# Engine programs emitted straight into the main program instead of inside a block

## The chip, the core and the metric

The kernel runs on one core of a Trainium2 chip. The core has five engines, each with its own instruction stream: the matrix engine (PE; its weight loads are shown as PEld), the vector engine (DVE), the scalar engine (ACT), GpSimd (POOL) and the sync engine (SP), which here issues nearly all transfers. The engines run by themselves and wait for each other through semaphores. The metric is the device time of one execution of the program in microseconds, as the median of several runs; lower is better.

## The reference

Sixteen tiles of 128 tokens (2048 tokens, width 512) go through two branches whose results are mixed by a gate. Branch A is attention with 32 heads of width 16 in four segments of 512 tokens, causal inside a segment, and a linear memory carried from one segment to the next. Branch B is a gated feed-forward layer with 1792 hidden units.

```python
x = A_x
g = _sigmoid((x * gate_w).sum(-1, keepdims=True))
a = _A_ref(x, A_wq, A_wk, A_wv, A_wo, A_beta)
b = _B_ref(x, B_W_gate, B_W_up, B_W_down)
return g * a + (1 - g) * b
...
for s in range(N):
    logits = jnp.einsum('bhqd,bhkd->bhqk', qs, ks) * scale + mask
    p = _softmax(logits, axis=-1)
    a_dot = jnp.einsum('bhqk,bhkd->bhqd', p, vs)
    pq = phi(qs)
    a_mem = num / den
    o = g * a_mem + (1.0 - g) * a_dot
    M = M + jnp.einsum('bhld,bhle->bhde', pk, vs)
    z = z + jnp.einsum('bhld->bhd', pk)
...
gate = gate * (gate > 0)
h = gate * up
return jnp.einsum('bsf,fd->bsd', h, W_down)
```

## The kernel before

The kernel is made in two steps. First `program` describes the whole computation as operations with the tiles that they read and write, and a list scheduler (`Sched.run`) decides, at build time, which engine does each operation and in which order; the outcome is one list per engine, `sc.prog[e]`, of two kinds of items: a wait for a semaphore's value, and an instruction that raises a semaphore when it is done. Second, `Sched.emit` walks the five lists and writes the instructions. All weights lie in SBUF; the four segments are worked through in order, with the projections (L791, L793), the attention scores and their weighted sums (L913, L969), the feed-forward products (L1043, L1082) and the output projection (L1075) interleaved on PE.

The change touches the second step alone. Before, `build_kernel` opens a block (L576) and hands it to `emit` (L577 calls it); `emit` gets one section of the block for each engine (`block.tensor`, `block.scalar` and so on) and writes each engine's list into its section (L540). What the reader needs of the surroundings:

- Ahead of the block stands an opening that every program of this kind has. It is attributed to L1188, where the program object is made: POOL sets four constants, every engine drains and raises one semaphore, POOL collects the four of them and raises another, and the four engines then go on.
- Entering the block gives each engine a jump from the main program to its own section (L540). Leaving the block gives each engine a jump to a common end section, and in it a closing meeting of the same make as the opening one: each engine drains and raises a semaphore, POOL waits for four of these and raises a second semaphore by four, and each of the others waits for one of the four. All of this is attributed to L576.
- The last thing in SP's list, written at the end of `program` (L1166 to L1168), is a wait for each of the 16 semaphores that count landed transfers. A wait is written by L534. Two waits fit in one instruction; in the kernel before, the sixteenth, for the semaphore of the last output store, is carried by SP's jump to the end section.
- The last stores to the output are issued by SP (L1094) from the tile `osb`, which ACT (L1092) and DVE (L1091) fill from the last products of PE (L1075, L1082).

Of the kernel before, what the change touches and what calls it, by code (L numbers as in the profile page):

```python
# [128 lines left out]
class Sched:  # L129
# [395 lines left out]
            self.place(op, e, start)  # L525
            self.relax = False

    def emit(self, block):
        sec = {"pe": block.tensor, "act": block.scalar, "dve": block.vector, "pool": block.gpsimd, "sp": block.sync}
        for e in self.ENGS:  # L530
            def body(engobj, prog=self.prog[e], e=e):
                for item in prog:
                    if item[0] == "wait":
                        engobj.wait_ge(self.sem[item[1]], item[2])  # L534
                    else:
                        _, op, st, inc = item
                        res = op.fns[e](engobj)
                        for r in (res if op.nd > 1 else [res]):
                            r.then_inc(self.sem[st], inc)
            sec[e](body)  # L540


def plan(S, D, F):
    NT, KT, NF = S // 128, D // 128, F // 128
    return [
        ("xT", [128, KT, XR * 512], BF16), ("wq", [128, KT, 512], BF16), ("wk", [128, KT, 512], BF16), ("wv", [128, KT, 512], BF16),
        ("wo", [128, 4, 512], BF16), ("wg", [128, KT, F], BF16), ("wu", [128, KT, F], BF16), ("wd", [128, NF - SBX, 512], BF16),
        ("qT", [128, QTN, 512], BF16), ("kT", [128, 4, 512], BF16), ("kp", [128, 5, 8, 128], BF16),
        ("phiq", [128, 4, 512], BF16), ("ek", [128, EKN, 512], BF16), ("phik", [128, 4, 512], BF16), ("ttmp", [128, 2, 512], BF16),
        ("vaug", [128, 2, 4, 32, 17], BF16), ("vsh", [128, 4, 32, 17], BF16), ("E", [128, NBLK * 512], BF16),  # L550
        ("Tn", [128, TNN, 512], F32), ("adT", [128, 512], BF16), ("oTt", [128, 512], BF16),
        ("amem", [128, 2, 512], BF16), ("amemT", [128, 4, 512], BF16), ("oT", [128, OTN, 512], BF16),
        ("hT", [128, HTN, 512], BF16), ("rl", [128, 3, 512], BF16), ("osb", [128, 3, 512], BF16),
        ("Mc", [128, 4, 68], F32), ("Mbd16", [128, 4, 136], BF16), ("mumask", [128, 4, 136], F32),
        ("braw", [128, 32], BF16), ("eb", [128, 32], F32), ("romgh", [128, 32], F32), ("epsv", [128, 32], F32),
        ("gexp", [128, NT], F32), ("omg", [128, NT], F32), ("gexpT", [128, NT * 4], F32), ("gwb", [128, 512], BF16),  ("gl", [128, NT], F32),
        ("rden", [128, 64], F32), ("rdg", [128, 64], F32), ("rdm", [128, 128], F32), ("pm8", [128, 8], F32), ("pm", [128, 2], F32), ("ident", [128, 128], BF16),
    ]


def build_kernel(nc, A_x, A_wq, A_wk, A_wv, A_wo, A_beta, W_g, W_u, W_d, gate_w, out):
    _, S, D = A_x.shape
    F = W_g.shape[1]
    assert D == 512 and S % 512 == 0 and F % 128 == 0
    NSEG, KT, NF, NT = S // 512, D // 128, F // 128, S // 128
    EPS, SCALE = 1e-6, 16 ** -0.5
    sc = Sched(seeds=(237719, 74891, 0, 89398, 0, 53401, 416309, 0, 0, 0, 710933, 0, 718714, 120896, 538430, 820480, 585027, 870794, 793690, 0, 589972, 0, 0, 0, 454998, 16783, 0,))
    T = {}
    with contextlib.ExitStack() as stack:
        for name, shape, dt in plan(S, D, F):  # L570
            T[name] = stack.enter_context(nc.sbuf_tensor(name, shape, dt))
        PS = stack.enter_context(nc.psum_tensor("ps", [128, 8, 512], F32))
        for st in sc.streams:
            sc.sem[st] = stack.enter_context(nc.semaphore(f"s_{st}"))
        program(sc, nc, T, PS, A_x, A_wq, A_wk, A_wv, A_wo, A_beta, W_g, W_u, W_d, gate_w, out, NSEG, KT, NF, NT, EPS, SCALE)
        with nc.Block() as block:  # L576
            sc.emit(block)  # L577
    return sc


# [590 lines left out]
def bass_gated_mix__memory_aug_infini_attn__glu_gated_reglu__prompt_kernel(  # L1171
    nc, A_x, A_wq, A_wk, A_wv, A_wo, A_beta, B_x, B_W_gate, B_W_up, B_W_down, gate_w, out
):
    return build_kernel(nc, A_x, A_wq, A_wk, A_wv, A_wo, A_beta, B_W_gate, B_W_up, B_W_down, gate_w, out)
# [28 lines left out]
```

## Time and profile before

| | before |
|---|---|
| median of three runs | 264.14 us |
| lowest, highest run | 264.01, 264.25 us |
| span of the profiled execution | 262.7 us |
| instructions recorded | 6432 |
| PE busy | 255.7 us, 97% of the span |
| ACT, DVE, POOL busy | 184.5, 179.1, 131.0 us |
| granted TensorE clock over the span | 1.000 |

The span reaches from the first to the last of the program's own instructions, the opening at L1188 and the closing at L576 included. What the launch does before and after it lies outside the span and inside the metric. Instructions of an engine's queue (waits, drains, jumps, transfers issued) have a `q` behind the engine's name and do not count as busy.

### The profile page before, as it was taken

The page shows a single profiled execution, that of the slowest core. Times are in us where ns is not written, and L with a number is a line of the kernel's source. Part 1 is how long each engine was busy: PE and PEld are TensorE (multiplying, and loading weights), DVE is VectorE, ACT ScalarE, POOL GpSimd, SP SyncE. Part 2 cuts the span into 40 slices and gives each one's busy share as a digit, 9 for nine tenths or more (in the row PEclk, how much of TensorE's full clock was granted, in tenths as well). Part 3 has the DMA queues.
Part 4 walks back from the last instruction along what each step waited for, and adds up shares of the span by engine and source line. Part 5 has one row for each costly group of instructions (what it writes and reads, how often), then busy time and mean ns, then how long its engine had stood idle before and what let it go on. Part 6 is the DMA issues. An engine that isn't in the chain of part 4 may idle for free.

```text
span 262.7 us, 6432 instructions
## 1 busy us (share of the span) xinstructions
PE 255.7 (97%) x2619; PEld 114.6 (44%) x2653; DVE 179.1 (68%) x356; ACT 184.5 (70%) x160; POOL 131.0 (50%) x295
## 2 busy tenths in 40 slices
PE   8999999999999999999999999999999999999996
PEld 5444443444443544334444544443444444344444
DVE  5488878789986587778788676757667716477600
ACT  4586689999789779785768787677777665676021
POOL 3036557564646466666555457836365354545100
PEclk9999999999999999999999999999999999999999
DMA  6989646930261134213040242010131101000011
GB/s 197 286 302 281 138 66 148 274 44 22 68 155 25 24 81 117 48 22 33 10 107 13 59 91 23 4 40 2 31 76 40 22 24 34 26 2 2 0 42 40
DMA packets 34925, 19.87 MB, mean 76 GB/s; under 512 B 24016, under 2 KB 34128, under 8 KB 34896
## 3 DMA queue, kind: packets, MB, share of 16 engines
q1 hardware_dynamic: 34800, 19.46, 30.4%
q8 instruction: 21, 0.34, 0.6%
q14 instruction: 8, 0.07, 0.1%
q10 hardware_dynamic: 96, 0.00, 0.0%
HBM read 10.40 MB, written 2.11 MB: 48 GB/s over the span
## 4 chain that ended last, share of the span: by engine, by line
PE 97%; issue 1%; DVE 1%
PE ps L1043 38%; PE ps L1082 19%; PE ps L793 11%; PE ps L913 9%; PE ps L969 6%; PE ps L791 5%; PE ps L1075 5%; PE ps L856 1%; PE ps L693 1%; PE ps L707 1%; PE ps L836 0%; DVE hT L1054 0%; DVE Tn L979 0%; DVE osb L746 0%; DVE osb L1091 0%
## 5 line engine op out<-in xcount | busy, mean ns | idle before, releaser
L935 POOL TENSOR_SCALAR_AFFINE_SELECT E<-E 64x256 bf16<-64x256 bf16 (+1 forms) x256 | 111.1, 445 | 111.9 <-ACT E L929 82.7
L929 ACT ACTIVATE E<-ps 128x2048 bf16<-128x2048 f32 x72 | 135.1, 1876 | 38.7 <-PE ps L913 38.6
L1043 PE MATMUL ps<-xT,wu 128*128 128x512 bf16 x213 | 57.2, 380 | 1.4 <-issue 1.3
L1043 PE MATMUL ps<-xT,wg 128*128 128x512 bf16 x219 | 57.7, 380 | 0.6 <-issue 0.3
L1082 PE MATMUL ps<-wd,hT 128*128 128x512 bf16 (+2 forms) x229 | 52.8, 367 | 0.9 <-issue 0.6
L1054 DVE TENSOR_TENSOR hT<-ps,rl 128x512 bf16<-128x512 f32 x56 | 38.5, 687 | 16.5 <-PE ps L1043 16.4
L1082 PEld LDWEIGHTS ps<-wd,hT 128*128 128x128 bf16 x238 | 21.4, 98 | 23.8 <-issue 2.4
L1043 PEld LDWEIGHTS ps<-xT,wg 128*128 128x128 bf16 x224 | 20.6, 98 | 25.7 <-issue 2.8
L1043 PEld LDWEIGHTS ps<-xT,wu 128*128 128x128 bf16 x224 | 20.1, 98 | 25.4 <-issue 3.5
L913 PE MATMUL ps<-qT,kp 32*128 32x192 bf16 (+7 forms) x512 | 28.6, 287 | 0.0
L979 DVE STREAM_TRANSPOSE Tn<-ps 128x512 f32<-128x512 f32 x32 | 21.3, 696 | 9.1 <-PE ps L969 9.1
L1052 DVE TENSOR_SCALAR rl<-ps 128x512 bf16<-128x512 f32 x30 | 20.7, 690 | 8.2 <-PE ps L1043 7.9
L1091 DVE TENSOR_SCALAR osb<-ps,omg 128x512 bf16<-128x512 f32 (+1 forms) x8 | 5.6, 700 | 26.0 <-PE ps L1082 15.1
L1051 ACT ACTIVATE rl<-ps 128x512 bf16<-128x512 f32 x26 | 15.5, 598 | 9.9 <-PE ps L1043 9.7
L913 PEld LDWEIGHTS ps<-qT,kp 32*128 32x128 bf16 x512 | 8.2, 92 | 25.3 <-issue 13.1
L969 PE MATMUL ps<-E,vaug 64*17 64x128 bf16 (+7 forms) x512 | 18.7, 283 | 0.0
L969 PE MATMUL ps<-E,vsh 64*17 64x128 bf16 (+7 forms) x512 | 18.3, 283 | 0.0
L1092 ACT ACTIVATE osb<-ps,omg 128x512 bf16<-128x512 f32 (+1 forms) x9 | 6.1, 675 | 16.4 <-PE ps L1075 14.0
L793 PE MATMUL ps<-xT,wq 128*128 128x512 bf16 x61 | 16.1, 391 | 0.4 <-issue 0.3
L1075 PE MATMUL ps<-wo,oT 128*128 128x512 bf16 (+2 forms) x67 | 16.2, 366 | 0.2 <-issue 0.2
L793 PE MATMUL ps<-xT,wk 128*128 128x512 bf16 x60 | 15.6, 380 | 0.4 <-issue 0.3
L791 PE MATMUL ps<-wv,xT 128*128 128x512 bf16 x63 | 15.3, 380 | 0.1
(68 smaller groups left out, 229.2 us busy)
## 6 DMA issues: line engine op xcount, KB each, us to landing
vsh<-vaug SPq DMA_DIRECT2D x8, 272.0 KB, 4.3
osb<-in_A_x_dram SPq DMA_DIRECT2D x16, 128.0 KB, 2.3
out_dram<-osb SPq DMA_DIRECT2D x15, 128.0 KB, 1.7
wg<-in_B_W_gate_dram SPq DMA_DIRECT2D x8, 224.0 KB, 5.0
wu<-in_B_W_up_dram SPq DMA_DIRECT2D x8, 224.0 KB, 5.9
wd<-in_B_W_down_dram SPq DMA_DIRECT2D x1, 1792.0 KB, 10.5
hT<-in_A_x_dram SPq DMA_DIRECT2D x2, 256.0 KB, 3.0
wq<-in_A_wq_dram SPq DMA_DIRECT2D x4, 128.0 KB, 3.3
```

Of the source, the lines that this page charges most:

```text
L791: ins = e.matmul(A(ep)[:, :], lhsT=V.xT[:, kt, tok + col * 128:tok + (col + 1) * 128], rhs=w[:, kt, :], start=(kt == 0), stop=(kt == KT - 1))
L793: ins = e.matmul(A(ep)[:, :], lhsT=w[:, kt, col * 128:(col + 1) * 128], rhs=V.xT[:, kt, tok:tok + 512], start=(kt == 0), stop=(kt == KT - 1))
L913: ins = q.matmul(dst, lhsT=V.kp[r, kslot(s, G), c, :], rhs=V.qT[r, qslot(s, G), q0:q0 + w], start=True, stop=True, tile_position=(32 * jj, ...
L929: acts.append(act(lambda a: a.activation(V.E[:, base * 512:base * 512 + min(2048, 4 * W)], PF[:, 0:min(2048, 4 * W)], ACT.Exp, scale=SCALE ...
L935: pools.append(pool(lambda g, ap=ap, lim=lim, pat=pat: g.affine_select(out=ap, in_=ap, compare_op=ALU.is_ge, fill=0.0, base=lim, pattern=[ ...
L969: ins = q.matmul(A(eps[p])[32 * jj:32 * jj + 17, 64 * (c + u):64 * (c + u + n)], lhsT=v[:, 8 * G + 2 * jj + p, :], rhs=V.E[r, f:f + 64 * n ...
L979: ds.append(dve(lambda e, p=p, ep=eps[p]: e.transpose(V.Tn[:, 2 * (G % (TNN // 2)) + p, :], A(ep)[:, :]), t_dve(512), writes=[f"Tn{2 * (G ...
L1043: ins = e.matmul(A(ep)[:, :], lhsT=w[:, kt, f * 128:(f + 1) * 128], rhs=V.xT[:, kt, c % XR * 512:(c % XR + 1) * 512], start=(kt == 0), sto ...
L1052: ("dve", lambda e, ep=eg, r=r: e.tensor_scalar(V.rl[:, r, :], A(ep)[:, :], 0.0, None, ALU.max), t_dve(512))],
L1054: evs.append(dve(lambda e, ep=eu, r=r, hs=hs: e.tensor_tensor(V.hT[:, hs, :], A(ep)[:, :], V.rl[:, r, :], ALU.mult), t_dve(512), reads=[f" ...
L1075: ins = e.matmul(A(ep)[:, 0:c1 - c0], lhsT=V.oT[:, ot[G], i * 128:(i + 1) * 128], rhs=V.wo[:, G, c0:c1], start=st_ and G == 0, stop=sp_ an ...
L1082: ins = e.matmul(A(ep)[:, 0:c1 - c0], lhsT=V.hT[:, slots[f], i * 128:(i + 1) * 128], rhs=V.wd[:, f, c0:c1], start=st_ and f == f0, stop=sp ...
```

## The change

Each engine's instructions are written straight into the main program, one engine after the other, through the program's own engine objects (`nc.tensor`, `nc.scalar` and so on). There is no block, so there are no sections, no jumps to them and from them, and no end section with its drains and semaphores. The opening stays. The lists themselves, their order and their waits are the same; PE's products, for one, stand in the same order. SP's 16 last waits now fill eight instructions, two in each, since there is no jump to carry the odd one.

```diff
@@ -525,8 +525,8 @@
-    def emit(self, block):
-        sec = {"pe": block.tensor, "act": block.scalar, "dve": block.vector, "pool": block.gpsimd, "sp": block.sync}
+    def emit(self, nc):
+        sec = {"pe": nc.tensor, "act": nc.scalar, "dve": nc.vector, "pool": nc.gpsimd, "sp": nc.sync}
         for e in self.ENGS:
             def body(engobj, prog=self.prog[e], e=e):
                 for item in prog:
@@ -537,7 +537,7 @@
                         res = op.fns[e](engobj)
                         for r in (res if op.nd > 1 else [res]):
                             r.then_inc(self.sem[st], inc)
-            sec[e](body)
+            body(sec[e])
@@ -573,8 +573,7 @@
         for st in sc.streams:
             sc.sem[st] = stack.enter_context(nc.semaphore(f"s_{st}"))
         program(sc, nc, T, PS, A_x, A_wq, A_wk, A_wv, A_wo, A_beta, W_g, W_u, W_d, gate_w, out, NSEG, KT, NF, NT, EPS, SCALE)
-        with nc.Block() as block:
-            sc.emit(block)
+        sc.emit(nc)
     return sc
```

Since one line goes, lines behind the block have numbers lower by one in the changed kernel.

## The prediction, written before the changed kernel was run

> **What bounds the kernel now.** I read four views, from the whole to the end. First the profile's page: its span and the chain that ended last.
>
> ```profile
> span 262.7 us, 6432 instructions
> ...
> PE 97%; issue 1%; DVE 1%
> ```
>
> PE is the bound nearly from the first to the last microsecond. None of its instructions is added, taken away or moved, so the change can earn or lose only at the two ends, before PE's first product and after its last, and in how the instructions arrive. So the second view is the chain of waits over the last microseconds (start, length, what).
>
> ```profile
> 260.24 0.24 PE ps L1075 x4
> 260.48 0.02 issue
> 260.50 0.35 DVE osb L1091
> ```
>
> PE's last four products end at 260.5, DVE makes the last 128 columns of the output by 260.85, and from there no engine computes. What fills the rest shows in the instructions of the output stores (L1094) from 260.85 on and in what SP waited for.
>
> ```profile
> L1094 SPq DMA_DIRECT2D out_dram<-osb x1: 332/332/332, 260.9 to 260.9; - x1
> ...
> DMA to landing us min/median/max: 1.5/1.5/1.5
> ```
>
> ```profile
> SPq L576 <- DMA out_dram<-osb: 0.6, 1, 0.6
> SPq L576 <- PEq L576: 0.2, 1, 0.2
> ```
>
> The last store is issued at 260.9 and needs 1.5 us, so it lands at about 262.3 to 262.4. SP stands on it for 0.6 us, and then for another 0.2 us on something that is no transfer: the closing meeting. The fourth view has all instructions of that meeting (durations in ns as min/median/max, then first and last start).
>
> ```profile
> L576 POOLq EVENT_SEMAPHORE  x2: 17/17/17, 262.6 to 262.6; - x2
> L576 POOLq DRAIN  x1: 509/509/509, 243.4 to 243.4; - x1
> L576 PEldq DRAIN  x1: 1195/1195/1195, 259.3 to 259.3; - x1
> L576 ACTq DRAIN  x1: 612/612/612, 259.5 to 259.5; - x1
> L576 DVEq DRAIN  x1: 393/393/393, 260.5 to 260.5; - x1
> L576 SPq COMPARE_BRANCH  x1: 41/41/41, 262.3 to 262.3; - x1
> L576 SPq DRAIN  x1: 7/7/7, 262.5 to 262.5; - x1
> L576 SPq EVENT_SEMAPHORE  x1: 17/17/17, 262.7 to 262.7; - x1
> L576 ACTq EVENT_SEMAPHORE  x1: 17/17/17, 262.7 to 262.7; - x1
> L576 DVEq EVENT_SEMAPHORE  x1: 21/21/21, 262.7 to 262.7; - x1
> L576 PEldq EVENT_SEMAPHORE  x1: 51/51/51, 262.7 to 262.7; - x1
> ```
>
> Read it in time: POOL is through at 243.4 + 0.5 = 243.9, ACT at 260.1, PE at 260.5, DVE at 260.9. SP's jump to the end section, which carries the wait for the last store, runs at 262.3; SP drains at 262.5; POOL collects and releases at 262.6; everybody leaves at 262.7, where the span ends. So the last 0.4 us of the span (262.3 to 262.7) are the meeting and the jump to it, and nothing lies under them.
>
> **The change part by part.** The sum is made against the profiled execution: its span of 262.7 and what the launch does around it, for which the page has no row. The median of the runs, 264.14, stands 264.14 - 262.7 = 1.4 us above that span; I take these 1.4 us as what lies around it and subtract from 264.14.
>
> *The closing meeting (five drains and six semaphore instructions) and SP's jump.* All of it after the last landing goes, and it is the very end of the path: 262.7 - 262.3 = 0.4 us. Both times are rounded to a tenth, so the difference is 0.3 to 0.5. In its place comes the rest of SP's last wait. SP's waits from the list are these:
>
> ```profile
> L534 SPq EVENT_SEMAPHORE  x13: 17/28/59, 29.1 to 261.7; - x13
> ```
>
> The eight that end the list took 17 to 59 ns each and the last began at 261.7, before the landing. In the changed kernel the eighth holds two semaphores, the last store's among them, so it starts at 261.7, stands until 262.3 and ends at most 0.06 us later. I count -0.4 and keep -0.3 and -0.5 as ends. What is late next is nothing of the program: SP's last wait ends it, and the four other engines' drains were done by 260.9.
>
> *Jumps into the sections (five, L540), and the four jumps out that carry no wait.* The trace has no record of them:
>
> ```profile
> nothing on L540; most used: ['L969', 'L913', 'L1043', 'L1082', 'L935', 'L793', 'L836', 'L534', 'L1075', 'L791', 'L856', 'L929', 'L1054', 'L619', 'L707', 'L746', 'L979', 'L1052', 'L1051', 'L810', 'L693', 'L798', 'L1188', 'L1094', 'L743']
> ```
>
> That alone could mean that they aren't recorded, but SP's jump at L576 is, so I believe that they cost nothing as they lead only to the next instruction. The bound: each engine leaves the opening meeting at 0.7 (rows of L1188) and does its first work soon after (timeline: start, length).
>
> ```profile
> L1188 SPq DRAIN  x1: 7/7/7, 0.0 to 0.0; - x1
> ...
> L1188 POOLq DRAIN  x1: 188/188/188, 0.4 to 0.4; - x1
> ...
> L1188 SPq EVENT_SEMAPHORE  x1: 17/17/17, 0.7 to 0.7; - x1
> L1188 ACTq EVENT_SEMAPHORE  x1: 17/17/17, 0.7 to 0.7; - x1
> L1188 DVEq EVENT_SEMAPHORE  x1: 21/21/21, 0.7 to 0.7; - x1
> L1188 PEldq EVENT_SEMAPHORE  x1: 51/51/51, 0.7 to 0.7; - x1
> ```
>
> ```profile
> 0.80 0.20 POOL L670 MEMSET ident<- 128x128 bf16 x1 [0.29 <-POOLq L1188]
> 0.81 1.28 ACT L646 ACT_TABLE_LOAD   x1 [0.81 <-PEq L1188]
> 0.81 0.87 SPq L619 DMA_DIRECT2D hT<-in_A_x_dram  x2
> ...
> 3.69 0.56 PEld L707 LDWEIGHTS ps<-ident,hT 128*128 128x128 bf16 x6 [0.18 <-DMA hT<-in_A_x_dram]
> ```
>
> SP issues its first load at 0.81, about 0.1 us after its release, and PE's first real work at 3.69 waits 0.18 us for that load: whatever SP gained here would come through. It can't be more than the 0.1 us, less what an instruction needs anyway; a loss has no place there, as nothing is added. I take 0.
>
> *The body.* Same lists, same waits, same queues; no DMA is issued earlier or past another, and no wait is added behind which something would queue. 0. Its cover is the fetching of instructions ahead of use, which the streams' new layout could in principle uncover:
>
> ```profile
> q8 instruction: 21, 0.34, 0.6%
> ```
>
> 21 packets took 0.6% of 16 engines' span, 0.006 x 16 x 262.7 = 25 us, so about 1.2 us each. One that came late by its whole length would cost PE 1.2 us.
>
> *What lies around the span.* After its last instruction each engine goes on into the launch's own closing, and the execution can't be over before all five have come through. Before, all five leave the meeting at 262.7 and start on that way together; after, four start on it at 243.9 to 260.9, and SP alone at 262.3. So whatever is slow there for an engine other than SP gets hidden. The trace shows no row of that code. The nearest row is how far apart the engines come out of the launch's code at the start: SP drains at 0.0, and POOL at 0.4 with 0.19, so by 0.6 (MOVE and four constants of its own ahead of it, so the true spread is less). A gain of 0.6 is the far end, and 0 the near one, if SP is itself the slowest; SP has waits and transfers only and was the first to come out, so I take the middle, -0.3.
>
> On this the Trainium skill speaks, in "Runtime: NRT & Kernel Launch", "The ~15µs preamble/postamble breakdown": behind a kernel the runtime puts a barrier of its own in which all engines are waited for, given there as about 1.5 us. By that rule the meeting removed here was a second one and nothing needs it; no row of this trace shows that barrier, whose figure is near the 1.4 us above. If all of its length were waiting for engines other than SP, the sum would be 264.14 - 0.4 - 1.5 = 262.2; I don't use it, as part of it must be the hand-over itself.
>
> Sum: 264.14 - 0.4 - 0 - 0 - 0.3 = 263.44, say 263.45, 0.26% less. By its ends: 264.14 - 0.5 - 0.1 - 0.6 = 262.9 and 264.14 - 0.3 = 263.8.
>
> **The rivals.**
>
> *Only the span gets shorter.* SP is on its own way out as late as the slowest engine was before, or it is first in an order in which the engines then meet, so that the rest follows it in turn as before. Then 264.14 - 0.4 = 263.74, 0.15% less. For it: SP is the last to arrive in both kernels. Against it: the four others have nothing of their own left to do by then.
>
> *Nothing to be seen.* The launch's closing has a fixed pace of its own, set by something that neither kernel touches, and takes up the 0.4 us: 264.1. Against it: the program's end releases it, and the end comes earlier.
>
> *Slower: a late instruction packet.* The streams lose their jumps, and so each packet boundary falls on another instruction than before. If one packet of PE then comes when PE has run dry, PE stands for up to 1.2 us at a place where it bounds everything: 264.14 - 0.4 + 1.2 = 264.94. It decides from a stall of 0.4 us up. For it: PE is busy 97% of the time, so nothing absorbs a stall. Against it: the shift is a few instructions in a stream that 21 packets carry, and the issue share of the chain is 1% in all.
>
> *A fetch goes with the jumps.* The same page of the Trainium skill ("Instruction fetch mechanics") says that a taken branch breaks the sequential prefetch and stalls for a fetch when the target isn't at hand; by that rule the change would win more. As a mechanism here: one packet of 1.2 us less on the way to the first load, 264.14 - 0.4 - 1.2 = 262.5. Against it: the 0.1 us between release and first load has no room for a packet, and SP's one recorded jump took 41 ns and was followed by its drain 0.2 us later (262.3, 262.5).
>
> **How the numbers follow.** The forecast 263.45 has a chance of 0.60, with 263.0 to 263.65 as its own range; only the span shorter 0.28; nothing seen 0.04; slower 0.05; more by a fetch 0.03. The range for 8 in 10 takes in the forecast's ends and the first rival's: 263.0 to 263.95, leaving out the slower case, "nothing seen" and the fetch, and little more. What a measurement of this kernel can tell from no change is about 0.2%, 0.53 us, so faster means below 263.61. Of the forecast's 0.60 some 0.06 lie above that; of the first rival's 0.28 (half of a tenth off 263.74 either way) some 0.03 lie below. Faster: 0.54 + 0.03 + 0.03 = 0.60. Within: 0.06 + 0.25 + 0.04 = 0.35. Slower: 0.05.
>
> **What would show it.** In the changed profile: a span of 262.3 (262.2 to 262.4); no drain, semaphore or jump behind SP's last wait, and that wait beginning at about 261.7 and lasting to 262.3; the first load still issued at 0.8; PE's busy time and its chain the same to 0.1 us. The second term shows only in the runs: the median less the span, now 1.4, should be 1.1. If it stays at 1.4, the first rival holds. I am wrong in the main step if the span does not fall by 0.3 to 0.5, and wrong in the body if PE shows idle time, ended by "issue", that was not there.

## The result and the profile after

The changed kernel takes 263.5 us (median of 16 runs, 262.97 to 264.16), the kernel before 264.19 us in the runs beside it (16 runs, 263.86 to 265.13). The ratio is 0.9971 with a 95% interval of 0.9961 to 0.998, that is 0.77 us less (0.53 to 1.03). The two medians are 0.69 us apart; the ratio is not their quotient. The forecast was 263.45.

The page of the changed kernel, where the first row is the span and the third the engines' shares of the chain that ended last:

```profile
span 262.3 us, 6420 instructions
...
PE 255.7 (97%) x2619; PEld 114.7 (44%) x2653; DVE 179.5 (68%) x356; ACT 184.5 (70%) x160; POOL 130.7 (50%) x295
...
PE 97%; issue 1%; DVE 1%
```

PE's busy time is 255.7 us in both; the span is 0.4 us shorter. The end of the chain of waits (start, length, what), and the last output store:

```profile
260.19 0.24 PE ps L1074 x4
260.43 0.03 issue
260.45 0.35 DVE osb L1090
```

```profile
L1093 SPq DMA_DIRECT2D out_dram<-osb x1: 332/332/332, 260.8 to 260.8; - x1
...
DMA to landing us min/median/max: 1.5/1.5/1.5
```

PE's last products begin at 260.19 instead of 260.24, within what one execution differs from another, and the store again needs 1.5 us. What follows the landing is new. First what SP waited for in the last 8 us, then SP's waits as a group (durations in ns as min/median/max, first and last start):

```profile
SPq L1093 <- ACT osb L1091: 6.0, 2, 3.5
SPq L534 <- DMA out_dram<-osb: 0.6, 1, 0.6
SPq L1093 <- DVE osb L1090: 0.4, 1, 0.4
```

```profile
L534 SPq EVENT_SEMAPHORE  x13: 17/28/567, 28.9 to 261.7; - x13
```

The wait for the store is now an ordinary wait of the list. It begins at 261.7, is the one of 567 ns, and the span ends with it at 262.3. The other 0.2 us that SP had to wait at L576 has no row any more. The traces hold their times finer than these views print them: the last store lands at 262.33 before and at 262.28 after; the span ended 0.41 us behind the landing before, and ends 0.02 us behind it now.

The beginning, in order of time:

```profile
0.81 0.86 SPq L618 DMA_DIRECT2D hT<-in_A_x_dram  x2
...
3.74 0.56 PEld L706 LDWEIGHTS ps<-ident,hT 128*128 128x128 bf16 x6 [0.23 <-DMA hT<-in_A_x_dram]
```

SP's first load is issued at 0.81 as before, so the jumps into the sections had cost nothing that this trace can show.

Each of these runs of the changed kernel, and each run of the experiments, comes with its own span. Over the 16 runs of the changed kernel the span lies between 261.7 and 262.9, but the time less the span is always 1.21 to 1.27, median 1.25. In 30 runs of the kernel before, beside the first experiments, it is 1.67 to 1.77, median 1.72, while the spans lie between 262.0 and 263.3. (Over all 81 such runs, on three chips, it is 1.67 to 1.79, with medians of 1.72, 1.73 and 1.74 by chip, so it can be compared from chip to chip.) The span is given to a tenth, so each difference is good to 0.05. This difference separates the two kernels in every run, where a single time does not, and the experiments below are read by it.

### The profile page after: what moved, and what is told of

It is laid out like the page before. It is cut to its first block, busy times and chain, and to the rows that moved or that the text cites. A ratio compares the mean times of both kernels' runs of the same rounds, so it can differ in the third digit from the quotient of the medians.

```text
span 262.3 us, 6420 instructions
## 1 busy us (share of the span) xinstructions
PE 255.7 (97%) x2619; PEld 114.7 (44%) x2653; DVE 179.5 (68%) x356; ACT 184.5 (70%) x160; POOL 130.7 (50%) x295
## 4 chain that ended last, share of the span: by engine, by line
PE 97%; issue 1%; DVE 1%
PE ps L1042 38%; PE ps L1081 19%; PE ps L792 11%; PE ps L912 9%; PE ps L968 6%; PE ps L790 5%; PE ps L1074 5%; PE ps L855 1%; PE ps L692 1%; PE ps L706 1%; PE ps L835 0%; DVE hT L1053 0%; DVE Tn L978 0%; DVE osb L745 0%; DVE osb L1090 0%
## 5 line engine op out<-in xcount | busy, mean ns | idle before, releaser
L968 PEld LDWEIGHTS ps<-E,vaug 64*17 64x17 bf16 x512 | 11.6, 86 | 8.5 <-issue 4.4
```

What stands on the lines that cost most here:

```text
L968: ins = q.matmul(A(eps[p])[32 * jj:32 * jj + 17, 64 * (c + u):64 * (c + u + n)], lhsT=v[:, 8 * G + 2 * jj + p, :], rhs=V.E[r, f:f + 64 * n ...
```

## The experiments

The theory was: the change is worth the closing meeting and SP's jump inside the span, and outside it that four engines get early to the launch's own closing. The rivals: it is the jumps and sections; or only the span got shorter. All experiments start from the changed kernel.

**One meeting put back by hand.**

```diff
-        sc.emit(nc)
+        sc.emit(nc); nc.all_engine_barrier()
```

> The changed kernel with the closing meeting of the five engines put back by hand behind SP's last wait, and still no block and no jumps. Theory: the whole change is this meeting, 0.3 to 0.35 us in the span (0.4 less SP's jump and its drain) and the rest around the span, since the four other engines again leave together at the end. So the span is 0.3 to 0.35 above the changed kernel's, the time less the span goes from about 1.25 to about 1.7, and the time is that of the kernel before within 0.15 us. Rival (jumps and sections cost the larger part): the time stays within 0.35 us of the changed kernel, and the time less the span stays at 1.25.

264.11 us, against 264.37 of the kernel before on the same chip; the ratio is 1.0001 (0.999 to 1.0012). The time was expected within 0.15 us of the kernel before: the ratio says so, the medians, 0.26 us apart, do not; so far does the scatter of the spans move a median. The time less the span is 1.73. SP's waits from the list, and the meeting's rows:

```profile
L534 SPq EVENT_SEMAPHORE  x13: 17/28/569, 29.0 to 261.5; - x13
```

```profile
L576 POOLq EVENT_SEMAPHORE  x2: 17/17/17, 262.1 to 262.2; - x2
L576 POOLq DRAIN  x1: 507/507/507, 243.1 to 243.1; - x1
...
L576 SPq DRAIN  x1: 7/7/7, 262.1 to 262.1; - x1
L576 SPq EVENT_SEMAPHORE  x1: 17/17/17, 262.2 to 262.2; - x1
...
L576 PEldq EVENT_SEMAPHORE  x1: 51/51/51, 262.3 to 262.3; - x1
```

From SP's drain at 262.1 to the span's end at 262.3 it takes 0.2 us, as in the kernel before (262.5 to 262.7). What differs lies ahead of the drain. By the traces' own times it follows the landing by 0.06 us here, with nothing but the end of SP's wait of 569 ns between them, and by 0.19 us in the kernel before, where SP's jump, the only one of the ten that was recorded, stood between them. The span ends 0.28 us behind the landing here, 0.41 in the kernel before and 0.02 in the changed kernel, so in the span the meeting costs 0.26 us and the jump 0.13. The meeting alone brings back everything outside the span, so the jumps and sections are not the larger part. How much longer than the changed kernel's its span is could not be told from the spans themselves, since no run of the changed kernel stands beside it and the spans scatter.

**No meeting, but the other four engines kept until the last store has landed too.**

```diff
             sc.prog["sp"].append(("wait", f"dma{i}", sc.semval[f"dma{i}", sc.cnt[f"dma{i}"]]))
+    last = Q["spo"][-1]
+    for e in ('pe', 'act', 'dve', 'pool'):
+        sc.prog[e].append(("wait", last.stream, sc.semval[last.stream, last.idx]))
```

> The changed kernel in which PE, ACT, DVE and POOL each wait for the last output store too, as SP does, before they end; no meeting. Theory: the span stays as in the changed kernel (to 0.1 us), but all five start on the launch's closing together at about 262.3, so the time less the span rises from 1.25 to about 1.75, and the time by 0.5 us. Rival (only the span got shorter, the engines' way out is not hidden by ending early): the time less the span stays at 1.25 to 1.3 and the time is that of the changed kernel within 0.1 us.

264.17 us (ratio to the kernel before 0.9988, 0.9977 to 0.9999); the time less the span is 1.73, as with the meeting, though nobody meets anybody. So it is not the meeting that costs this 0.48 us outside the span. It is that the four other engines end late.

**One late engine at a time.** The same edit with one engine in the list.

> The changed kernel in which POOL alone waits for the last output store too; PE, ACT and DVE end early as in the changed kernel. Theory, sharpened: POOL is the engine with the longest way into the launch's closing, so it alone brings back nearly all of what lies around the span: time less span 1.65 to 1.8. Rival (all engines have the same way, or PE has the longest): time less span 1.25 to 1.45.

> The changed kernel in which PE alone waits for the last output store too; POOL, ACT and DVE end early. Theory with POOL the slow one: PE's lateness costs less than POOL's, time less span 1.3 to 1.6. Rival (PE is the slow one): time less span 1.7 and more, and POOL's late ending alone costs little.

> The changed kernel in which ACT alone waits for the last output store too. Theory (each engine that ends late adds what its own way into the launch's closing is longer than SP's; POOL 0.55 us, PE 0.25): ACT adds less than POOL, time less span 1.35 to 1.55. Rival (any second late engine adds the same, and POOL's excess is chance): 1.65 to 1.8.

> The changed kernel in which DVE alone waits for the last output store too. Theory: adds less than POOL and not more than ACT, time less span 1.25 to 1.5. Rival: as for ACT, 1.65 to 1.8.

| late besides SP | time less span, median (runs) | more than with SP alone |
|---|---|---|
| none (the changed kernel) | 1.25 (16) | |
| DVE | 1.36 (10) | 0.10 |
| ACT | 1.38 (10) | 0.12 |
| PE | 1.50 (12) | 0.25 |
| POOL | 1.80 (6) | 0.55 |
| all four | 1.73 (12) | 0.48 |
| the kernel before (meeting of five) | 1.72 (30) | 0.47 |

The times themselves do not show this order: 263.53 us with DVE late, 263.25 with ACT, 263.76 with PE, 263.63 with POOL, since the spans differ by more than the effects. DVE and ACT ran on another chip than PE and POOL; the kernel before differs by 0.01 us between the two in the time less the span.

The waits of the run in which POOL is late show how small the edit is: one wait more on POOL (44 for 43), begun at 261.8, when the store lands and SP's wait of 560 ns ends as well.

```profile
L534 POOLq EVENT_SEMAPHORE  x44: 17/17/17, 14.9 to 261.8; - x44
L534 SPq EVENT_SEMAPHORE  x13: 17/28/560, 29.0 to 261.2; - x13
```

POOL alone costs all that the four cost together. The amounts do not add up; the slowest one decides. (POOL alone shows slightly more than all four, 1.80 against 1.73. With all four late PE's last instruction, of 51 ns, ends the span 0.08 us behind the landing, with POOL alone its own, of 17 ns, 0.04 us behind it, which accounts for half of that; the rest is open.) The rival that any second late engine costs the same has fallen. Why POOL costs the most stays open: what it does behind the program may take longer, or the others may wait for it there in some fixed order. No row shows that code.

**A meeting without POOL.** If POOL's way out is what the meeting laid bare, a meeting of the other four should cost less outside the span.

```diff
-        sc.emit(nc)
+        sc.emit(nc); nc.multi_engine_barrier([nc.sync.engine, nc.tensor.engine, nc.scalar.engine, nc.vector.engine])
```

> The changed kernel with a closing meeting by hand of PE, ACT, DVE and SP behind SP's last wait; POOL is left out and ends early, ACT collects in its place. Theory: the meeting costs its hand-over of 0.2 to 0.3 us in the span as the one of five did, but around the span only what PE's lateness costs is paid, 1.50, not POOL's 1.73: time less span 1.4 to 1.55. Rival (it is the meeting, not the late engine, that brings back what lies around the span): 1.7 to 1.75.

263.84 us (ratio 0.9987, 0.9975 to 1.0). The time less the span is 1.57, just above the range expected and well below 1.73. The 0.07 us above the 1.50 of PE's late end are open; here ACT also collects in POOL's place. The meeting still costs its hand-over in the span, from SP's drain at 261.6 to 261.8:

```profile
L576 SPq DRAIN  x1: 7/7/7, 261.6 to 261.6; - x1
...
L576 PEldq EVENT_SEMAPHORE  x1: 51/51/51, 261.8 to 261.8; - x1
```

**Two meetings one behind the other.**

```diff
-        sc.emit(nc)
+        sc.emit(nc); nc.all_engine_barrier(); nc.all_engine_barrier()
```

> The changed kernel with two closing meetings by hand, one behind the other, no block and no jumps. Theory: a meeting costs its hand-over every time, 0.25 us (0.2 to 0.35) of span more than with one, and the engines' way out is paid once however many meetings there are: time less span stays at 1.73. Rival (the second meeting is free, since all engines are there already): the span behind SP's last wait is as long as with one meeting, 0.26 us.

264.46 us (ratio to the kernel before 1.0006, 0.9988 to 1.0024), time less span 1.72.

```profile
L576 SPq DRAIN  x2: 7/7/7, 262.1 to 262.3; - x2
L576 SPq EVENT_SEMAPHORE  x2: 17/17/17, 262.2 to 262.6; - x2
```

SP comes out of the first meeting at 262.2 and out of the second at 262.6; by the trace's own times 0.33 us go for a meeting in which all engines are already there. Outside the span nothing is added. The two terms are apart from each other: each meeting pays its own hand-over, the way out is paid once.

**A second meeting at the start, none at the end.**

```diff
-        sc.emit(nc)
+        nc.all_engine_barrier(); sc.emit(nc)
```

> The changed kernel with a second meeting by hand right behind the opening one, none at the end. Theory: the first load and the whole body shift by one hand-over, first load at 1.0 to 1.15 instead of 0.81, span 0.2 to 0.35 longer, and the time less span stays at 1.25, since the engines still end apart. Rival (a meeting anywhere brings back what lies around the span): time less span 1.7.

The time less the span is 1.24. The beginning in order of time:

```profile
1.13 0.39 SPq L618 DMA_DIRECT2D hT<-in_A_x_dram  x1
...
3.98 0.49 PEld L706 LDWEIGHTS ps<-ident,hT 128*128 128x128 bf16 x6
```

The first load goes out at 1.13 instead of 0.81, PE's first real work begins at 3.98 instead of 3.74. So a meeting at the start does not touch what lies outside the span, and it does shift the start by a quarter of a microsecond. That this makes the whole longer by as much could not be told: 263.72 us, ratio to the kernel before 0.9972 (0.9954 to 0.999), with spans that scatter by 0.4 us (standard deviation of 10 runs) and no run of the changed kernel on that chip.

**The changed kernel again**, beside the meeting without POOL.

> The changed kernel once more, beside the one before and the meeting without POOL on the same chip. Theory: span 0.4 us below the kernel before (to 0.15), time less span 1.25 against 1.72, so the time 0.85 us lower (0.65 to 1.05). Rival (what the 16 runs showed is all there is, 0.69): 0.5 to 0.7 lower.

263.35 against 264.28 us: 0.93 less, ratio 0.9965 (0.9949 to 0.998). The median span is 262.1 against 262.5, the time less the span 1.24 against 1.74. The two terms, 0.4 and 0.5, make up the difference. The interval still holds 0.69, so the rival is not excluded by the times alone.

## Why the prediction was right

*The meeting and SP's jump, -0.4.* Right in place and size. What the span has behind the last landing went from 0.41 to 0.02 us. The medians of the span over runs on one chip are 262.5 and 262.1. That the profiled spans, 262.7 and 262.3, differ by just 0.4 is in part luck: a single span of the changed kernel could have been any from 261.7 to 262.9. The last wait begins at 261.7 and ends the span, as forecast. What the prediction did not part: 0.26 us is the hand-over, 0.13 us the jump that carried the wait.

*The jumps into the sections, 0.* Right. The first load is issued at 0.81 in both. The rival of a fetch that goes with the jumps, drawn from a page of the Trainium skill ("Runtime: NRT & Kernel Launch", "Instruction fetch mechanics"), has fallen with it: no time was gained at the start.

*The body, 0.* Right: PE busy 255.7 us in both, and the share of "issue" in the chain is 1% in both. Even that 1% is no stall: both traces lack records of 34 of PE's 2653 products, and the trace of the run with ACT late, which has them all, shows PE 99% and issue 0%. The slower rival, a late instruction packet, did not show.

*What lies around the span, -0.3.* The mechanism was right and both numbers were too small. The term itself is 1.72 - 1.25 = 0.47 us, inside the bounds of 0 and 0.6 and above the middle that I took between them. And "these 1.4 us as what lies around it" was mis-sized: it set the median of three runs against the span of a single execution, and to 264.14 belongs a span of about 264.14 - 1.72 = 262.4, not 262.7; run by run it is 1.72. By the sign that the prediction gave, the median less the one profiled span, the change would have shown 263.5 - 262.3 = 1.2, between the 1.1 of the forecast and the 1.4 of the first rival, and decided little. The total of the two terms is 0.39 + 0.47 = 0.86 where the forecast had 0.7. The measured medians differ by 0.69 in the first comparison and by 0.93 in the second, both with intervals that hold 0.86, so that the forecast comes within 0.05 us of the result is luck: the scatter of the spans made up for the term that was too small. (A slip beside it: the range's lower bound of 263.0 does not take in the forecast's own lower end, 262.9.)

*The reason for it* was stated as "whatever is slow there for an engine other than SP gets hidden". The runs name the engine: POOL, 0.55 us longer than SP when it is late alone. The choice of the middle rested on how far apart the engines come out of the launch at the start (SP at 0.0, POOL's drain at 0.4); that row pointed to the right engine and nearly to the right size, but by luck. POOL's first instruction there is a MOVE at 0.1, ahead of the four constants, and the engine that comes last is PE:

```profile
L1188 POOLq MOVE  x1: 39/39/39, 0.1 to 0.1; - x1
...
L1188 PEldq DRAIN  x1: 8/8/8, 0.3 to 0.3; - x1
```

No run shows that the way out follows the order of the way in.

*Only the span gets shorter* has fallen: it needs 1.72 outside the span in both kernels, and the changed kernel has 1.25. The rule of the Trainium skill on the runtime's own barrier behind a kernel ("Runtime: NRT & Kernel Launch", "The ~15µs preamble/postamble breakdown") fits what the runs show but is not needed for it: if each engine had its own way out and the execution ended with the last of them, the runs would look the same. No view used here has a row of that barrier, and its figure of about 1.5 us was not a saving to be had: 1.25 us stay outside the span with SP alone at the end.

## What to carry to other kernels

A closing meeting at the end of a program costs twice: its own hand-over of some 0.3 us (0.4 with SP's jump here), and the head start that engines already done would have had on the launch's closing (0.5 us here). Let each engine simply end, and let only the one engine that has to see the last transfer land wait for it; of the choices tried, SP alone was the cheapest, and POOL the worst engine to be late. SP waited to the end in all of them, so whether another engine alone in its place would be cheaper is not known. When an effect is below the scatter of the spans, compare the time less the span run by run and what the trace shows behind the last landing, and don't take a median over runs against one profiled span.

## What was not expected of the hardware

The span of one and the same program differs from run to run by more than the whole effect: 261.7 to 262.9 us in 16 runs of the changed kernel. In the profiles the last store was issued between 260.1 (the meeting without POOL) and 261.5 (PE late), so most of it arises ahead of the tail. The twelve traces show where: PE's 801st weight load starts between 88.4 us (the meeting without POOL) and 89.8 us (PE late), and the last one 171.0 us later in every trace. So the scatter comes from the first 90 us, and from there on PE's work repeats to 0.01 us. What differs in the first part was not followed further; in the longest of the twelve, PE late, PE waits there for 0.4 us for a load of xT, which it does not in the changed kernel's trace. A meeting that every engine has already reached is not free: the second of two costs 0.33 us.
